# The last stage of a fused attention and two-layer kernel: two double steps split into single ones, two weight tiles loaded ahead, a new order

## The chip, the cores and the metric

The kernel runs on one core of a Trainium2 chip. The engines are named as in the profile: PE (TensorE, matrix products; PEld its weight loads), DVE (VectorE), ACT (ScalarE), POOL (GpSimd), and SP, whose queue issues the DMAs. The metric is the device time of one launch in microseconds (us): before the change 757.48 us, the median of three runs (756.21 to 758.75).

## The reference

Three stages follow one another: pooled attention, a soft mixture of experts, and a two-layer network with a bend between its layers. Only the last is touched:

```python
def _moe2_ref(x, w_in, w_out):          # x: 2304 x 512
    h = x @ w_in                        # w_in: 512 x 2048
    g = h - np.tanh(h)
    return (g @ w_out).astype(np.float32)   # w_out: 2048 x 512
```

The mixture before it gives `x = c @ slot_out` with 32 slots, so the kernel folds `slot_out @ w_in` into a 32-row matrix first, and h is c times that.

## The kernel before

**Tiling of the last stage.** The 2304 tokens are taken in 6 blocks of 384 (`TB`), the 2048 hidden columns in 16 tiles f of 128. A step is a block and two neighbouring tiles (`NF = 2`): 48 double steps. In the sequence `seq` they are numbered n = 0 to 47; the first block holds n = 0 to 7, the second begins with n = 8.

**One double step.** PE makes h for the two tiles (`fh`, line 1460, two products of 384 columns into one of two PSUM banks `h`). ACT reads h three times: its square u (`fu`, 1467), its tanh th (`ft`, 1470) and a mask big (`fb`, 1473), and makes y from u (`fy`, 1476). DVE multiplies u by th (`fm`, 1481), subtracts th from h (`fd`, 1484), makes a polynomial for small h (`fg`, 1487) and chooses between the two (`fp`, 1492). ACT rounds the result to gh (`fa`, 1495), DVE makes the remainder gl (`fl`, 1498). PE then adds to the three output tiles of the block (`acc`, 128 tokens each) the products gh with the upper half of a weight tile (o0), gh with its lower half (o1), and gl with the upper half (o2): 18 products of 512 columns (`fo`, line 1505). All five DVE instructions and all five ACT instructions of a double step are 768 columns wide. After the last step of a block an output tile is copied out by ACT or by DVE, whichever the planner finds free (`fe`, 1542 and 1544), and stored through SP (`fs`, 1548). The buffers u, y, m, th, big, gh and gl have three copies each, the banks h two, and there are four output accumulators, where a block needs three.

**What the later steps wait for.** The folded matrix (`s0`, `s1`) holds 16 tiles. Its first four come ready with the work just ahead (lines 1385 and 1386). The twelve others are made by `slot_rest` (line 1316: 24 products that read the converted weights i0 to i5), rounded by `s4` on ACT (1404), their remainder taken by `s5` on DVE (1407), and put in place by twelve small DMAs `s6` (1421): so h for f of 4 and above (`sw_done`) needs that whole chain. Only after all of the s6 does `reload` fetch the tiles 4 to 15 of the second weight.

**Loads ahead of it.** `top_up` (line 1082) hands memory that becomes free to the names in `wants`, in order, and issues the DMA that each needs: i0 to i5 at line 1103, the tiles of the second weight (numbers) at line 1105. c0 to c2, s0 and s1 are made on the chip and need none.

```python
wants = ["c0", "c1", "c2", "s0", "s1"] + [f"i{n}" for n in range(6)] + list(range(NF0))   # NF0 = 4
```

**Who sets the order.** `Plan.run` plays the stage through with a cost per operation and a delay between engines, at each free engine takes the ready operation with the lowest priority number, and writes the instructions in that order; on the chip each engine then runs its own list strictly in order. The priority is the step number plus an offset from `PO` by kind: h, u, t (th), b (big), y, m, d (th minus h), g, p, a (gh), l (gl), o0 to o2, ev (the copy out), r (slot_rest, s4, s5, s6). An operation that shares the bank h with another engine's (`alone`) waits until that one is done. `slot_rest` is held back until 4.0 us of planned time by `WAIT`.

```python
oh = op(pe(163 * NF), fh, q + PO["h"], deps=[...sw_done...], take=[hs], use=[hs])
om = op(dve(N), fm, q + PO["m"], deps=[ou, ot], take=[m], use=[u, th, m])
od = op(dve(N), fd, q + PO["d"], deps=[ot, om], use=[hs, th], alone=hs)
oe = op({**act(DM), **dve(DM)}, fe, q + PO["ev"], deps=outs[blk][t][-1:], take=[osb], use=[acc[t], osb])
```

Of the kernel before, what the change touches and what calls it, by code (L numbers as in the profile page):

```python
# [194 lines left out]
def fused_kernel(  # L195
# [12 lines left out]
    nc = tc.nc  # L208


    B, NP, _, S = q.shape
# [32 lines left out]
        "h": -8.11, "u": -2.9, "t": -2.69, "b": -2.37, "y": -2.66, "m": -13.37, "d": 0.89,  # L244
        "g": -5.49, "p": -3.56, "a": -1.55, "l": 2.75, "o0": 7.66, "o1": 8.11, "o2": 1.93,
        "ev": 5.8, "r": -0.78,
# [106 lines left out]
    def pe(ns):  # L353
        return {"PE": ns}
# [722 lines left out]
    wants = ["c0", "c1", "c2", "s0", "s1"] + [f"i{n}" for n in range(6)] + list(range(NF0))  # L1077
# [33 lines left out]
    with tc.manual_schedule():  # L1111
# [257 lines left out]
        seq = [(blk, f) for blk in range(NB) for f in range(0, KF, NF)]  # L1369
# [70 lines left out]
        def step(n):  # L1440
            blk, f = seq[n]
# [8 lines left out]
            def hp_():  # L1450
                return hs.tile[:, :, :TB]

            def v(sl, dt=None):
                t = sl.tile if dt is None else sl.tile.bitcast(dt)
                return t.rearrange("p (f c) -> p f c", f=NF)

            def fh(_):
                for k in range(NF):
# [16 lines left out]
            def fy(_):  # L1475
                nc.scalar.activation(
                    out=y.tile, in_=u.tile, func=AF.Square, scale=G_S, bias=gp[:, 0:1]
                )

            def fm(_):  # L1480
                nc.vector.tensor_tensor(out=m.tile, in0=u.tile, in1=th.tile, op=ALU.mult)  # L1481
# [4 lines left out]
            def fg(_):  # L1486
                nc.vector.scalar_tensor_tensor(
                    out=m.tile, in0=y.tile, scalar=G_Q, in1=m.tile, op0=ALU.add, op1=ALU.mult
                )

            def fp(_):
                nc.vector.copy_predicated(m.tile, big.tile.bitcast(U32), th.tile)  # L1492

            def fa(_):
                nc.scalar.activation(out=hi.tile, in_=m.tile, func=AF.Copy)  # L1495

            def fl(_):
                nc.vector.tensor_tensor(  # L1498
                    out=lo.tile, in0=m.tile, in1=hi.tile.bitcast(F32), op=ALU.subtract
                )  # L1500

            def fo(k, t):
                for x in range(NF):
                    l, c = ((hi, 0), (hi, DM), (lo, 0))[k]
                    nc.tensor.matmul(  # L1505
                        out=acc[t].tile, lhsT=l.tile[:, x * TB + t * 128:x * TB + (t + 1) * 128],
                        rhs=got[f + x][:, c:c + DM], start=(f == 0 and k == 0 and x == 0),
                        stop=(f == KF - NF and k == 2 and x == NF - 1),
                    )

            q = float(n)
            N = NF * TB
            oh = op(pe(163 * NF), fh, q + PO["h"], deps=[d for x in range(NF) for d in sw_done[f + x]],
# [11 lines left out]
            for k in range(3):  # L1525
                for t in range(NTB):
                    done = outs[blk][t]
                    deps = [ol if k == 2 else oa] + done[:1]
                    if f == KF - NF and k == 2:
                        deps += done  # L1530
                    o = op(pe(215.7 * NF), lambda _, k=k, t=t: fo(k, t),
# [4 lines left out]
            if f == KF - NF:  # L1536
# [73 lines left out]
```

## Time and profile before

| | |
|---|---|
| median of three runs | 757.48 us |
| profiled execution, its own time | 755.35 us |
| its span, first to last instruction | 753.6 us |
| PE busy | 726.4 us, 96% of the span |
| DVE busy | 652.8 us, 87% |
| ACT busy | 485.9 us, 64% |
| mean granted TensorE clock | 0.989 of full |
| start of the last stage (first h) | 519.39 us |
| last product of the last stage ends | 749.84 us |

The shares of the whole span hide that its stages differ; the last stage is 230 us of 753.6 and has to be read by itself. A window table gives the busy time of every engine in a stretch; the granted clock beside it says at which of its two levels (1.0 is 2.4 GHz, 0.5 is 1.2 GHz) PE worked there. The timeline lists the instructions by their start; neighbours of one kind are merged into one row, and the bracket at its end says how long the engine had been idle and what it waited for.

### The profile page before, as it was taken

How to read it: one execution, taken by the hardware profiler on the slowest of the kernel's cores; microseconds unless marked ns; L12 is line 12 of the kernel's file. 1: busy time of each engine (PE TensorE's matmuls, PEld its weight loads, DVE VectorE, ACT ScalarE, POOL GpSimd, SP SyncE). 2: the span in 40 equal slices, each digit the busy share in tenths (PEclk: the TensorE clock that was granted, in tenths of full speed). 3: DMA queues.
4: the chain of work that ended last, by engine and by line, in shares of the span. 5: the costliest groups of instructions: out<-in, count | busy, mean ns of one | idle time of the engine just before them, and what ended most of it. 6: DMA issues, size and time to landing. Idle time of an engine off the chain costs nothing.

```text
span 753.6 us, 16227 instructions
## 1 busy us (share of the span) xinstructions
PE 726.4 (96%) x5977; PEld 512.1 (68%) x5977; DVE 652.8 (87%) x1161; ACT 485.9 (64%) x1050; POOL 379.8 (50%) x275
## 2 busy tenths in 40 slices
PE   6999999999999989999989999998899999999998
PEld 3666666666666656666656666355678888888886
DVE  7999989898999999998989986513999999999994
ACT  1565666565666565666556666314878888888882
POOL 2699999969999869999939960000000000000000
PEclk9999999999999999999989999999799999999999
DMA  6445373453454444464444532999631010101001
GB/s 219 151 159 160 141 230 122 143 152 112 164 182 147 145 154 164 154 205 146 168 171 183 174 140 97 356 409 371 232 145 42 1 43 0 43 1 42 8 35 42
DMA packets 33551, 108.41 MB, mean 144 GB/s; under 512 B 5312, under 2 KB 6208, under 8 KB 33472
## 3 DMA queue, kind: packets, MB, share of 16 engines
q1 hardware_dynamic: 33472, 107.37, 40.5%
q8 instruction: 47, 0.77, 0.4%
q14 instruction: 32, 0.26, 0.1%
HBM read 90.24 MB, written 16.25 MB: 141 GB/s over the span
## 4 chain that ended last, share of the span: by engine, by line
PE 83%; DVE 7%; ACT 3%; POOL 3%; issue 2%; DMA 1%; SPq 0%; DVEq 0%; POOLq 0%; ACTq 0%
PE bk L1505 26%; PE bk L556 21%; PE bk L590 18%; PE bk L464 7%; POOL rt L609 3%; DVE mc L478 2%; PE h L1460 2%; PE bk L633 2%; PE bk L1330 2%; PE bk L1251 2%; DMA rt<-in_moe_w_in_dram 1%; PE bk L699 1%; PE bk L805 1%; PE bk L809 0%; DMA rt<-in_k_dram 0%
## 5 line engine op out<-in xcount | busy, mean ns | idle before, releaser
L609 POOL TENSOR_TENSOR rt<-rt 128x576 f32<-128x576 f32 x240 | 355.7, 1486 | 49.0 <-ACT rt L568 34.5
L568 ACT ACTIVATE rt<-bk 128x288 f32<-128x288 f32 x576 | 204.0, 412 | 147.1 <-PE bk L556 138.2
L478 DVE TENSOR_REDUCE mc<-bk 128x1 f32<-128x384 f32 x480 | 234.4, 546 | 26.3 <-PE bk L464 25.6
L556 PE MATMUL bk<-rt 64*128 64x288 f32 x1728 | 179.3, 310 | 4.8 <-DVE mc L478 4.6
L590 PE MATMUL bk<-rt 128*64 128x288 f32 x1152 | 173.3, 419 | 0.0
L556 PEld LDWEIGHTS bk<-rt 64*128 64x128 f32 x1728 | 138.8, 187 | 47.5 <-DVE mc L478 18.9
L1505 PE MATMUL bk<-rt,gh 128*128 128x512 f32 x576 | 145.3, 396 | 5.0 <-ACT gh L1495 5.0
L1505 PEld LDWEIGHTS bk<-rt,gh 128*128 128x128 f32 x576 | 109.4, 191 | 29.2 <-ACT gh L1495 6.7
L590 PEld LDWEIGHTS bk<-rt 128*64 128x64 f32 x1152 | 70.1, 136 | 55.7 <-issue 25.9
L464 PE MATMUL bk<-rt 64*128 64x384 f32 x480 | 100.1, 395 | 7.9 <-DVE rt L414 7.0
L556 PE MATMUL bk<-rt,one 64*128 64x288 f32 x576 | 91.0, 294 | 0.0
L464 PEld LDWEIGHTS bk<-rt 64*128 64x128 f32 x480 | 54.5, 194 | 47.3 <-issue 18.9
L1505 PE MATMUL bk<-rt,gl 128*128 128x512 f32 x288 | 81.8, 395 | 0.0
L1505 PEld LDWEIGHTS bk<-rt,gl 128*128 128x128 f32 x288 | 54.4, 191 | 9.9 <-DVE gl L1498 0.6
L556 PEld LDWEIGHTS bk<-rt,one 64*128 64x128 f32 x576 | 60.1, 187 | 0.0
L1467 ACT ACTIVATE u<-h 128x768 f32<-128x768 f32 x48 | 39.2, 816 | 27.9 <-PE h L1460 27.9
L1492 DVE COPY_PREDICATED m<-big,th 128x768 f32<-128x768 uint32 x48 | 51.4, 1070 | 0.0
L1481 DVE TENSOR_TENSOR m<-u,th 128x768 f32<-128x768 f32 x48 | 45.6, 951 | 6.4 <-ACT th L1470 6.3
L417 DVE TENSOR_TENSOR rt<-rt 128x576 fp32r<-128x576 f32 (+3 forms) x35 | 47.0, 1343 | 4.4 <-ACT rt L412 4.3
L1498 DVE TENSOR_TENSOR gl<-m,gh 128x768 fp32r<-128x768 f32 x48 | 45.7, 952 | 1.5 <-ACT gh L1495 1.5
L1484 DVE TENSOR_TENSOR th<-h,th 128x768 f32<-128x768 f32 x48 | 45.6, 951 | 0.0
L1495 ACT ACTIVATE gh<-m 128x768 fp32r<-128x768 f32 x48 | 40.9, 852 | 7.3 <-DVE m L1492 5.0
(136 smaller groups left out, 695.6 us busy)
## 6 DMA issues: line engine op xcount, KB each, us to landing
rt<-in_moe_w_dram SPq DMA_DIRECT2D x64, 512.0 KB
rt<-in_v_dram SPq DMA_DIRECT2D x16, 576.0 KB
rt<-in_k_dram SPq DMA_DIRECT2D x15, 576.0 KB
rt<-in_q_dram SPq DMA_DIRECT2D x15, 576.0 KB
rt<-in_moe_w_in_dram SPq DMA_DIRECT2D x16, 512.0 KB
rt<-in_moe_w_out_dram SPq DMA_DIRECT2D x16, 512.0 KB
wo_hl<-rt SPq DMA_DIRECT2D x16, 512.0 KB
rt<-wo_hl SPq DMA_DIRECT2D x16, 512.0 KB
```

The lines of the kernel that those rows point to most:

```text
L417: nc.vector.tensor_tensor(out=lo_t[:, c:end], in0=sl.tile[:, c:end], in1=hi_t.bitcast(F32)[:, c:end], op=ALU.subtract,)
L464: nc.tensor.matmul(out=ps.tile[:, :KW], lhsT=QH[a][lo:hi, q0:q0 + 128], rhs=KH[a][lo:hi, c0:c0 + KW],)
L478: nc.vector.tensor_reduce(out=msl.tile[:, n, g:g + 1], in_=ps.tile[:, :KW], axis=AX.X, op=ALU.max)
L556: nc.tensor.matmul(out=st.tile[:, :HQ], lhsT=w[lo:hi, k0:k0 + 128], rhs=x[lo:hi, q], start=(n == 0), stop=(n == 3),)
L568: nc.scalar.activation(out=psl.tile[:, h, :], in_=st.tile[:, :HQ], func=AF.Exp, scale=ESC)
L590: nc.tensor.matmul(out=pvs.tile[lo:hi, :HQ], lhsT=vt[:, cc, h, :], rhs=p.tile[:, h, :], start=(cc == 0), stop=(cc == NCH - 1),)
L609: eng.tensor_tensor(out=acc.tile, in0=p0.tile if c == 1 else acc.tile, in1=psl.tile, op=ALU.add)
L1481: nc.vector.tensor_tensor(out=m.tile, in0=u.tile, in1=th.tile, op=ALU.mult)
L1484: nc.vector.tensor_tensor(out=v(th), in0=hp_(), in1=v(th), op=ALU.subtract)
L1492: nc.vector.copy_predicated(m.tile, big.tile.bitcast(U32), th.tile)
L1498: nc.vector.tensor_tensor(out=lo.tile, in0=m.tile, in1=hi.tile.bitcast(F32), op=ALU.subtract)
L1505: nc.tensor.matmul(out=acc[t].tile, lhsT=l.tile[:, x * TB + t * 128:x * TB + (t + 1) * 128], rhs=got[f + x][:, c:c + DM], start=(f == 0 an ...
```

## The change

Four things change, all of them for the last stage.

- The sequence: the first double step (block 0, tiles 0 and 1) becomes two single ones, the last (block 5, tiles 14 and 15) as well: 50 steps for 48. A single step has instructions of 384 columns on ACT and DVE and takes nine output products. The priority's step number is now the position in hidden tiles divided by two, so the two singles stand at 0 and 0.5.
- In `wants`, the tiles 0 and 1 of the second weight come ahead of i0 to i5.
- The offsets `PO` are all new.
- The planner's cost of a product goes from 163 to 172 ns (h) and from 215.7 to 227 ns (o).

```diff
     PO = {
-        "h": -8.11, "u": -2.9, "t": -2.69, "b": -2.37, "y": -2.66, "m": -13.37, "d": 0.89,
-        "g": -5.49, "p": -3.56, "a": -1.55, "l": 2.75, "o0": 7.66, "o1": 8.11, "o2": 1.93,
-        "ev": 5.8, "r": -0.78,
+        "h": 0.13, "u": -2.03, "t": -15.26, "b": -1.63, "y": -11.63, "m": -23.28, "d": 13.36,
+        "g": 3.69, "p": -8.99, "a": -7.63, "l": 4.72, "o0": 6.44, "o1": 8.34, "o2": 7.72,
+        "ev": 15.23, "r": -0.3,
     }
...
-    wants = ["c0", "c1", "c2", "s0", "s1"] + [f"i{n}" for n in range(6)] + list(range(NF0))
+    wants = ["c0", "c1", "c2", "s0", "s1", 0, 1] + [f"i{n}" for n in range(6)] + list(range(2, NF0))
...
-        seq = [(blk, f) for blk in range(NB) for f in range(0, KF, NF)]
+
+        seq = [(blk, f, NF) for blk in range(NB) for f in range(0, KF, NF)]
+        seq = [(0, 0, 1), (0, 1, 1)] + seq[1:-1] + [(NB - 1, KF - 2, 1), (NB - 1, KF - 1, 1)]
...
-            q = float(n)
-            N = NF * TB
-            oh = op(pe(163 * NF), fh, q + PO["h"], deps=[d for x in range(NF) for d in sw_done[f + x]],
+            q = float(blk * KF + f) / NF
+            oh = op(pe(172 * nf), fh, q + PO["h"], deps=[d for x in range(nf) for d in sw_done[f + x]],
...
-                    o = op(pe(215.7 * NF), lambda _, k=k, t=t: fo(k, t),
+                    o = op(pe(227 * nf), lambda _, k=k, t=t: fo(k, t),
                            q + PO[f"o{k}"] + (2 if n == len(seq) - 1 else 0.01) * t, deps=deps,
```

The rest of the diff makes the instructions of a step as wide as the step (`N = nf * TB` columns of the same buffers).

## Rows read from the trace of the kernel before

**Rows 1.** The page, part 1: busy time and share of the span by engine.
```profile
PE 726.4 (96%) x5977; PEld 512.1 (68%) x5977; DVE 652.8 (87%) x1161; ACT 485.9 (64%) x1050; POOL 379.8 (50%) x275
```
**Rows 2.** Chain of waits, last stage: start us, us, what.
```profile
622.79 0.35 PE h L1460 x2
623.14 4.10 PE bk L1505 x18
...
733.03 16.81 PE bk L1505 x74
```
**Rows 3.** Windows, last stage: stretch, its length, busy by engine, clock, DMA share, GB/s.
```profile
519.39:526.80 7.41, 5.72 (x30) 2.31 (x30) 5.47 (x8) 7.09 (x11) 0.00 (x0) 1.00 0.89 352
526.80:540.77 13.97, 11.27 (x42) 8.80 (x42) 13.39 (x16) 10.94 (x16) 0.00 (x0) 0.88 0.52 152
540.77:554.34 13.57, 11.97 (x37) 8.30 (x37) 12.71 (x15) 10.39 (x15) 0.00 (x0) 0.75 0.91 367
554.34:743.60 189.26, 189.26 (x850) 158.34 (x851) 184.23 (x208) 159.34 (x217) 0.00 (x0) 1.00 0.06 22
```
**Rows 4.** Windows of line 1505 alone (PE, PEld, clock, DMA, GB/s).
```profile
554.34:749.90 195.56, 188.33 (x798) 149.19 (x798) 1.00 0.06 22
```
**Rows 5.** Timeline, 519 to 546 us: start, us, engine, line, operation, count, idle before.
```profile
519.39 0.66 PE L1460 MATMUL h<-rt 128*128 128x384 f32 x2
...
520.82 3.99 PE L1316 MATMUL bk<-rt,acc_s 128*32 128x512 f32 x24
...
522.50 0.18 PEld L1316 LDWEIGHTS bk<-rt,acc_s 128*32 128x32 f32 x3 [0.25 <-DMA rt<-wi_c]
...
524.74 0.61 PE L1460 MATMUL h<-rt 128*128 128x384 f32 x2
...
526.82 1.20 PE L1505 MATMUL bk<-rt,gh 128*128 128x512 f32 x4 [1.48 <-ACT gh L1495]
...
527.26 8.22 SPq L1421 DMA_DIRECT2D rt<-sh  x12
...
528.58 1.01 PE L1460 MATMUL h<-rt 128*128 128x384 f32 x2 [0.56 <-DVE th L1484]
...
531.10 0.68 DVE L1407 TENSOR_TENSOR sh<-bk,sh 96x512 fp32r<-96x512 f32 x1
...
535.53 9.63 SPq L1105 DMA_DIRECT2D rt<-wo_hl  x12
...
536.41 0.51 PE L1460 MATMUL h<-rt 128*128 128x384 f32 x2
...
544.92 0.88 ACT L1495 ACTIVATE gh<-m 128x768 fp32r<-128x768 f32 x1
```
**Rows 6.** Windows, all engines: the DMA-bound stretch and the two at half clock.
```profile
504.00:525.00 21.00, 19.14 (x408) 13.76 (x398) 5.97 (x15) 5.80 (x10) 0.00 (x0) 1.00 1.03 408
...
528.35:531.65 3.30, 3.07 (x8) 2.60 (x9) 3.30 (x5) 2.36 (x4) 0.00 (x0) 0.50 0.43 99
541.97:548.39 6.42, 6.05 (x13) 4.18 (x14) 6.41 (x9) 6.07 (x9) 0.00 (x0) 0.50 1.03 416
```
**Rows 7.** Timeline, a settled step: m of one double step and of the next.
```profile
721.71 0.95 DVE L1481 TENSOR_TENSOR m<-u,th 128x768 f32<-128x768 f32 x1
...
726.14 0.94 DVE L1481 TENSOR_TENSOR m<-u,th 128x768 f32<-128x768 f32 x1
```
**Rows 8.** Groups by line and shape: 384 columns on DVE and on ACT.
```profile
L417 DVE TENSOR_TENSOR rt<-rt 128x384 fp32r<-128x384 f32 x3 | 1.7, 559 | 4.4 <-ACT rt L412 4.3
...
L412 ACT ACTIVATE rt<-rt 128x384 fp32r<-128x384 f32 x3 | 1.6, 522 | 1.9 <-DMA rt<-in_k_dram 1.8
```
**Rows 9.** Timeline: the last stores.
```profile
719.29 31.53 SPq L1548 DMA_DIRECT2D out_dram<-osb  x4
```
**Rows 10.** Groups by line: the copy out, on ACT and on DVE.
```profile
L1544 ACT ACTIVATE osb<-bk 128x512 f32<-128x512 f32 x17 | 9.7, 612 | 6.4 <-PE bk L1505 6.4
...
L1542 DVE COPY osb<-bk 128x512 f32<-128x512 f32 x1 | 0.7, 673 | 0.0
```

More of the change, by code (lines that the diff above doesn't have):

```diff
@@ L1440, in step @@
         def step(n):
-            blk, f = seq[n]
+            blk, f, nf = seq[n]
+            N = nf * TB
             hs = hbank()
@@ L1450, in hp_, with w @@
             def hp_():
-                return hs.tile[:, :, :TB]
+                return hs.tile[:, :nf, :TB]
             def v(sl, dt=None):
                 t = sl.tile if dt is None else sl.tile.bitcast(dt)
-                return t.rearrange("p (f c) -> p f c", f=NF)
+                return t[:, :N].rearrange("p (f c) -> p f c", f=nf)
+            def w(sl, dt=None):
+                return (sl.tile if dt is None else sl.tile.bitcast(dt))[:, :N]
             def fh(_):
-                for k in range(NF):
+                for k in range(nf):
                     x = f + k
@@ L1476, in fy @@
                 nc.scalar.activation(
-                    out=y.tile, in_=u.tile, func=AF.Square, scale=G_S, bias=gp[:, 0:1]
+                    out=w(y), in_=w(u), func=AF.Square, scale=G_S, bias=gp[:, 0:1]
                 )
             def fm(_):
-                nc.vector.tensor_tensor(out=m.tile, in0=u.tile, in1=th.tile, op=ALU.mult)
+                nc.vector.tensor_tensor(out=w(m), in0=w(u), in1=w(th), op=ALU.mult)
             def fd(_):
@@ L1487, in fg @@
                 nc.vector.scalar_tensor_tensor(
-                    out=m.tile, in0=y.tile, scalar=G_Q, in1=m.tile, op0=ALU.add, op1=ALU.mult
+                    out=w(m), in0=w(y), scalar=G_Q, in1=w(m), op0=ALU.add, op1=ALU.mult
                 )
             def fp(_):
-                nc.vector.copy_predicated(m.tile, big.tile.bitcast(U32), th.tile)
+                nc.vector.copy_predicated(w(m), w(big, U32), w(th))
             def fa(_):
-                nc.scalar.activation(out=hi.tile, in_=m.tile, func=AF.Copy)
+                nc.scalar.activation(out=w(hi), in_=w(m), func=AF.Copy)
             def fl(_):
                 nc.vector.tensor_tensor(
-                    out=lo.tile, in0=m.tile, in1=hi.tile.bitcast(F32), op=ALU.subtract
+                    out=w(lo), in0=w(m), in1=w(hi, F32), op=ALU.subtract
                 )
             def fo(k, t):
-                for x in range(NF):
+                for x in range(nf):
                     l, c = ((hi, 0), (hi, DM), (lo, 0))[k]
@@ L1507, in fo @@
                         rhs=got[f + x][:, c:c + DM], start=(f == 0 and k == 0 and x == 0),
-                        stop=(f == KF - NF and k == 2 and x == NF - 1),
+                        stop=(f + nf == KF and k == 2 and x == nf - 1),
                     )
-            q = float(n)
-            N = NF * TB
-            oh = op(pe(163 * NF), fh, q + PO["h"], deps=[d for x in range(NF) for d in sw_done[f + x]],
+            q = float(blk * KF + f) / NF
+            oh = op(pe(172 * nf), fh, q + PO["h"], deps=[d for x in range(nf) for d in sw_done[f + x]],
                     take=[hs], use=[hs])
@@ L1528, in step @@
                     deps = [ol if k == 2 else oa] + done[:1]
-                    if f == KF - NF and k == 2:
+                    if f + nf == KF and k == 2:
                         deps += done
-                    o = op(pe(215.7 * NF), lambda _, k=k, t=t: fo(k, t),
+                    o = op(pe(227 * nf), lambda _, k=k, t=t: fo(k, t),
                            q + PO[f"o{k}"] + (2 if n == len(seq) - 1 else 0.01) * t, deps=deps,
@@ L1535, in step @@
                     done.append(o)
-            if f == KF - NF:
+            if f + nf == KF:
                 for t in range(NTB):
```

## The prediction

> **What bounds the kernel now.** I read the page first: PE is busy for 96% of the span [rows 1]. That is an average over stages, so the last stage comes next. Its chain of waits, from 554 us on, is PE alone, without a gap: 18 output products in 4.10 us (0.228 us each) and a pair of h products in 0.35 us, so 4.45 us per double step, up to the last product at 733.03 + 16.81 = 749.84 us [rows 2]. The windows say the same: in 554.34 to 743.60 PE is busy for 189.26 of 189.26 us [rows 3]. After 554.34 the stage can gain only if less PE work is left there. Of the 864 products 798 lie after that moment [rows 4], so only 66 are done in the first 35 us.
>
> How large is that loss? The stage's PE work at full speed is 864 x 0.228 = 196.8, 48 pairs x 0.345 = 16.6, and slot_rest 4.0 [rows 5], together 217.4 us. The stage took 749.84 - 519.39 = 230.4 [rows 2, 5]. So 13.0 us are lost, all in the ramp. Idle PE makes (7.41 - 5.72) + (13.97 - 11.27) + (13.57 - 11.97) = 6.0 of it [rows 3]. Half clock, 1.2 GHz in two stretches with 3.07 + 6.05 us of busy PE, makes half of that, 4.6 [rows 6]; both stretches follow idle time. The other 2.4 is products spaced wider than 0.228.
>
> Why the ramp starves is seen in the timeline [rows 5]. The first output product waits until 526.82 for gh, 7.4 us after the first h. The h for f = 4 comes only at 536.41: slot_rest runs at 520.82 to 524.81, the first s6 goes out at 527.26, the s5 that half of them need runs at 531.10, and the twelve take SP until 535.48. Meanwhile steps of the second block fill ACT and DVE (the h at 524.74, and one more), but three accumulators belong to the first block and only one is left for theirs. DVE is busy for 13.39 of 13.97 us there [rows 3], partly with results PE can't use yet, and the gh of f = 4 is ready only at 544.92 + 0.88 = 545.8.
>
> DVE is the second bound, and a close one. From one m to the next pass 726.14 - 721.71 = 4.43 us [rows 7], against PE's 4.45. It runs ahead now only because PE lost 13 us.
>
> **The change part by part.** All sums are in the time of the profiled execution, whose 755.35 us are 753.6 of span and 1.75 around it; it lies 2.1 below the median of the runs, and I carry the difference in us over to that median.
>
> *Two single steps at the start.* A DVE instruction of 384 columns takes 0.56 us and one of 768 0.95 [rows 7, 8]; on ACT a 384 takes 0.52 [rows 8] against 0.88 for a 768 [rows 5]. In the chain h, u, th, m, g, d, p, gh one h product goes (0.33), three ACT instructions lose 0.35 each and four DVE instructions 0.39: 2.9 us, so the first gh is ready near 524 rather than 526.8. It brings PE less than that, because slot_rest stands ahead of it in PE's list (next part). The price is more fixed time: back to back, a 768 on DVE takes 4.43 / 5 = 0.886 a piece, 0.07 less than its duration, so two halves take 2 x (0.56 - 0.07) - 0.89 = 0.09 more; ten such pairs (five each at start and end) are 0.9 us on DVE. ACT is idle for 30 of 189 us [rows 3] and hides its own. The bounds are 0 (pairs hidden where DVE idles) and 10 x (2 x 0.56 - 0.95) = 1.7.
>
> A rule speaks against it: the Trainium skill, VectorE: DVE Perf Modes, section on the TRN2 errata, says that each VectorE instruction pays a fixed latency once, and advises tiles of at least 512 elements; its (N + 151) / 0.96 ns gives 0.557 and 0.957 us, which agrees with 0.559 and 0.95 here. By it the ten pairs would cost 10 x 0.157 = 1.6 us in place of 0.9.
>
> *Two single steps at the end.* PE has the same 18 products there and is the bound; the copy out, the store and the 3.8 us from the last product to the end of the span stay. I cost it at nothing; if DVE is late at the end, half-size steps save up to about 1.5 us of the last chain (p, gh, gl halved), if not they cost the 0.45 already counted.
>
> *Two tiles loaded sooner.* The DMA engines are full from 504 to 525 us at 408 GB/s [rows 6], so what is put ahead of i0 to i5 delays them by 2 x 0.524 MB / 408 GB/s = 2.57 us. slot_rest waited for the last of them at 522.50 [rows 5]; now that is 525.07, and its end moves from 524.81 to 527.4. Nothing hides this from the s4-s5-s6 chain. In return tiles 0 and 1 are there before 524; where they were, they could have come close to that. So the edit by itself loses; bounds 0 (slot_rest is late for another reason) to 2.57, and I take 2.57. PE's list, by the planner's own costs, becomes: both single h, then the h of tiles 2 and 3 (the first bank comes free at about 2.9 us of planned time, slot_rest at 4.06), then slot_rest, then gh products of both singles. So PE idles from 520 to 523 and partly to 525, and from 527.4 on it has work.
>
> *The order.* Offsets -0.3 for s4 and s5 against 3.7 to 13.4 for g, l, d: s5 should follow s4 by one instruction, not by four. With s4 at 527.5 and s5 by 529.3, the first four s6 (0.6 us each, the order on SP unchanged) are out by 530.5. A DMA takes up to 753.6 - 750.82 + 0.33 = 3.1 us from issue to done, by the last store [rows 9]; a small one I put at 2.3. So h for f = 4 at about 533, bounds 532 and 536.5. By the planner's costs only one step of the second block now comes ahead of it. DVE then has, from 521.0: 4.9 (singles), 4.4 (tiles 2 and 3), 0.7 (s5), 4.4 (second block), 3.6 (m, g, d, p for f = 4), and ACT 0.9: gh of f = 4 near 540, where it was at 545.8. The reload begins at 528 + 12 x 0.61 = 535.3 as before, and its first two tiles land two tile times (2.6) and some 2 us later, at 539.9: the same moment. Until then PE has 36 + 6 products and five pairs of h, 11.3 us from 527.4, so it is busy until 538.7.
>
> *The sum.* At 540.0 there are 42 products and six pairs done. 822 x 0.228 + 42 x 0.345 = 201.7 are left: PE's end at 741.7. For half clock after the idle time near 521 I add 1.7 (half of a 3.3 us stretch; bounds 0 and 3.2, half of the longer one [rows 6]). DVE's own end: 521.0 + 48 x 4.43 + 0.9 + 0.7 + 3 idle in the ramp + 2 for the last products = 740.2. The two are now so close that each delay of either reaches PE, where the lead hid them: DVE's idle time in the settled part was 5.0 of 189 us [rows 3], and I let a third, 1.6, count. PE's end: 745.0, a gain of 4.8, say 5.0 us: 750.4 for a profiled execution, 757.48 - 5.0 = 752.5 for the median.
>
> **The rivals.**
>
> *The ramp only changes its shape.* If s5 keeps its old distance, the h for f = 4 follows slot_rest by 536.41 - 524.81 = 11.6 us: at 539.0, and gh 5.3 later (five DVE instructions and gh), at 544.3. PE then idles for 5 us, gets a second stretch of half clock (3.2), and ends at 544.3 + 201.7 + 3.2 = 749.2, with some of the 1.6 at 750: no change. For it: nothing of the chain is shortened but its priorities. Against it: s5 was delayed by four DVE instructions that now rank behind it.
>
> *DVE becomes the bound through the copies out* (slower). The new offset for ev, 15.23, ranks the copy of an output tile behind every ACT instruction of the next steps, but on DVE before d (13.36) of steps two and more ahead. A copy on DVE costs 0.67 [rows 10], and one of 18 was there. If all 18 went there, DVE would end at 740.2 + 18 x 0.67 = 752.3, with the hiccups at 753.9: 4.0 us slower, 761.5. It decides from (749.8 - 741.8) / 0.67 = 12 copies. Against it: ACT is free for 30 of 189 us, 0.7 per step [rows 3], and the planner takes whichever engine is free first.
>
> *The full gain.* If slot_rest isn't late (or gh of the singles goes ahead of it) and nothing stumbles, DVE's 740.2 is the end: 9.6 us faster, 747.9. Against it: DVE and PE would have to mesh for 48 steps with 0.02 us to spare in each.
>
> **How the numbers follow.** Forecast 0.55, the ramp of another shape 0.22, copies on DVE 0.17, full gain 0.06. What can be told from no change is 0.3%, 2.3 us. Forecast and full gain are faster: 0.61; the second is the same: 0.22; the third slower: 0.17. The forecast's own range, by its bounds (slot_rest 2.57, clock 3.2, hiccups 0 to 5), is 749.5 to 755.2. The range takes in most of the second case and the lower part of the slower one: 747.8 to 759.5.
>
> **What would show it.** Right: the first output product not before 527; s5 within 2 us of s4; h for f = 4 (the first after the s6) near 533; over 80 products done by 554; PE gapless from 541, its last product near 745. Wrong: slot_rest ending before 525.5 (the loads did not matter); gh of f = 4 after 543; DVE with more than a handful of copies; idle PE between 560 and 730 of more than 3 us in sum.

## The result, and the profile after

The change makes the kernel slower: 761.74 us (median of four runs; 761.10 to 762.10) against 758.05 of the kernel before, run beside it; ratio 1.0051, 95% interval 1.0031 to 1.0070. The forecast was 752.5 us, with a chance of 0.61 for faster.

The profiled execution took 761.54 us, 6.2 more than the 755.35 before. The first h of the last stage comes 3.4 us later (522.84 for 519.39), the stage takes 232.6 us for 230.4, and from its last product to the end of the span it is 4.4 us for 3.8. The 3.4 can't be put down to the change: the kernel before, profiled a second time (e0 below), had its first h at 521.17, and e17 below, which differs from it in the planner's costs alone, at 523.47.

The page of the changed kernel, part 1, beside [rows 1]: PE is busy 3.2 us longer for the same number of products.

```profile
PE 729.6 (96%) x5977; PEld 510.6 (67%) x5977; DVE 656.9 (86%) x1173; ACT 485.9 (64%) x1058; POOL 380.2 (50%) x275
```

Windows of its last stage, columns as in [rows 3]. The first three are the ramp, then two short stretches in it, and the part after the first 35 us.

```profile
522.84:532.46 9.62, 7.20 (x29) 2.77 (x29) 7.68 (x14) 7.54 (x15) 0.00 (x0) 0.82 0.63 251
532.46:543.20 10.74, 9.59 (x43) 7.65 (x43) 8.66 (x11) 8.90 (x13) 0.00 (x0) 1.00 0.41 104
543.20:554.94 11.74, 8.70 (x31) 6.57 (x31) 10.38 (x12) 8.16 (x12) 0.00 (x0) 0.85 0.99 384
528.00:530.00 2.00, 2.00 (x12) 0.95 (x9) 2.00 (x4) 2.00 (x4) 0.00 (x0) 0.50 0.38 147
548.00:551.00 3.00, 3.00 (x8) 2.33 (x8) 3.00 (x5) 1.06 (x2) 0.00 (x0) 0.50 1.01 408
...
557.80:755.39 197.59, 197.49 (x873) 160.91 (x871) 188.41 (x218) 160.91 (x225) 0.00 (x0) 1.00 0.06 22
```

In the ramp PE idles 2.42 + 1.15 + 3.04 = 6.6 us, as long as before (6.0), and again has two stretches at half clock. The last row is the surprise: PE looks busy for 197.49 of 197.59 us. The same window for line 1511 alone, the products, shows that it isn't well busy:

```profile
557.80:755.39 197.59, 187.84 (x793) 147.70 (x791) 1.00 0.06 22
```

793 products are left after 35 us, so 71 are done; before it was 66. At 0.2278 us a product and 0.345 us a pair of h (40 pairs, the other 80 PE instructions) the work is 180.65 + 13.80 = 194.45 us: 3.1 us are lost. The same sum for the kernel before, over 554.40 to 749.79 with the 798 products of [rows 4] and 39 pairs, gives 195.39 - 181.78 - 13.46 = 0.15. I call this figure the loss after 35 us. (The Trainium skill, Perfetto Trace Analysis, section Identifying the Most-Contended Engine, says that the busy share of the matmuls is not a good measure of how close a kernel is to roofline. This trace agrees: 99.9% busy, and 1.6% lost.) The chain of waits shows where it hides: beside the even 4.10 and 0.35 of [rows 2] stand pairs of h that take 0.53 and 0.58.

```profile
585.74 0.35 PE h L1466 x2
586.09 3.19 PE bk L1511 x14
589.28 0.53 PE h L1466 x2
589.80 7.29 PE bk L1511 x32
...
597.13 0.58 PE h L1466 x2
```

The waits from 557.8 on (us in total, times, the longest) name the cause of most: the weight load of h waits for the subtraction on DVE that frees its bank ("DVE th"), or it waits for nothing that the profile shows ("issue"), behind the 39 semaphore instructions that stand at this line.

```profile
PEld h L1466 <- issue: 3.2, 9, 0.4
...
PEld h L1466 <- DVE th L1490: 1.2, 4, 0.4
PEld bk L1511 <- DVE osb L1547: 0.5, 2, 0.3
...
```

The timeline of the ramp, beside [rows 5] (h of f = 4 is the one at 537.28, its gh the one at 545.99):

```profile
522.84 0.66 PE L1466 MATMUL h<-rt 128*128 128x384 f32 x2
...
525.91 0.62 PE L1466 MATMUL h<-rt 128*128 128x384 f32 x2 [2.42 <-DVE th L1490]
...
526.46 6.06 PE L1316 MATMUL bk<-rt,acc_s 128*32 128x512 f32 x24
...
527.21 0.38 PEld L1316 LDWEIGHTS bk<-rt,acc_s 128*32 128x32 f32 x6 [0.60 <-DMA rt<-wi_c]
...
532.46 1.65 PE L1511 MATMUL bk<-rt,gh 128*128 128x512 f32 x6
532.56 0.60 ACT L1406 ACTIVATE sh<-bk 96x512 fp32r<-96x512 f32 x1 [2.07 <-PE bk L1316]
533.18 7.63 SPq L1423 DMA_DIRECT2D rt<-sh  x12
533.19 0.69 DVE L1409 TENSOR_TENSOR sh<-bk,sh 96x512 fp32r<-96x512 f32 x1 [1.23 <-ACT sh L1406]
...
537.28 0.53 PE L1466 MATMUL h<-rt 128*128 128x384 f32 x2
...
543.20 0.62 PE L1466 MATMUL h<-rt 128*128 128x384 f32 x2 [1.15 <-DVE th L1490]
...
545.99 0.85 ACT L1501 ACTIVATE gh<-m 128x768 fp32r<-128x768 f32 x1
...
546.72 0.72 PE L1511 MATMUL bk<-rt,gl 128*128 128x512 f32 x2 [1.98 <-DVE gl L1504]
```

PE waits for DVE at the third h, slot_rest stands behind that h and runs partly at half clock (6.06 us for 3.99), s5 makes DVE wait 1.23 us for s4, and after 542 PE stands still three more times.

### The profile page after: what moved, and what is told of

Same layout as the page of the kernel before. It is cut to its first block, busy times and chain, and to the rows that moved or that the text cites. A ratio compares the mean times of both kernels' runs of the same rounds, so it can differ in the third digit from the quotient of the medians.

```text
span 759.8 us, 16244 instructions
## 1 busy us (share of the span) xinstructions
PE 729.6 (96%) x5977; PEld 510.6 (67%) x5977; DVE 656.9 (86%) x1173; ACT 485.9 (64%) x1058; POOL 380.2 (50%) x275
## 4 chain that ended last, share of the span: by engine, by line
PE 42%; DMA 5%; DVE 3%; ACT 2%; issue 1%; ACTq 0%; DVEq 0%; SPq 0%
PE bk L1511 25%; PE bk L556 5%; PE bk L590 5%; DMA rt<-in_moe_w_dram 4%; PE h L1466 2%; PE bk L464 1%; DMA rt<-wi_c 1%; PE bk L1316 1%; DVE mc L478 1%; PE bk L1251 1%; PE bk L633 1%; PE bk L805 0%; PE bk L809 0%; ACT th L1476 0%; DVE m L1487 0%
## 5 line engine op out<-in xcount | busy, mean ns | idle before, releaser
L478 DVE TENSOR_REDUCE mc<-bk 128x1 f32<-128x384 f32 x480 | 234.7, 549 | 28.4 <-PE bk L464 27.8
L1511 PEld LDWEIGHTS bk<-rt,gh 128*128 128x128 f32 x576 | 107.8, 189 | 24.6 <-ACT gh L1501 1.4
L464 PEld LDWEIGHTS bk<-rt 64*128 64x128 f32 x480 | 55.2, 194 | 46.9 <-issue 20.6
L1511 PE MATMUL bk<-rt,gl 128*128 128x512 f32 x288 | 80.1, 395 | 2.0 <-DVE gl L1504 2.0
L1476 ACT ACTIVATE th<-h 128x768 f32<-128x768 f32 (+1 forms) x50 | 39.7, 797 | 26.3 <-PE h L1466 26.1
L417 DVE TENSOR_TENSOR rt<-rt 128x576 fp32r<-128x576 f32 (+3 forms) x35 | 48.8, 1396 | 4.6 <-ACT rt L412 4.5
L1498 DVE COPY_PREDICATED m<-big,th 128x768 f32<-128x768 uint32 (+1 forms) x50 | 50.5, 1032 | 0.0
L1487 DVE TENSOR_TENSOR m<-u,th 128x768 f32<-128x768 f32 (+1 forms) x50 | 45.9, 918 | 3.2 <-ACT u L1473 2.2
L1504 DVE TENSOR_TENSOR gl<-m,gh 128x768 fp32r<-128x768 f32 (+1 forms) x50 | 45.5, 917 | 2.7 <-ACT gh L1501 2.7
L1482 ACT ACTIVATE y<-u,gp 128x768 f32<-128x768 f32 (+1 forms) x50 | 46.5, 930 | 0.0
L1490 DVE TENSOR_TENSOR th<-h,th 128x768 f32<-128x768 f32 (+1 forms) x50 | 45.0, 918 | 1.3
```

Source lines behind the costliest of these rows:

```text
L417: nc.vector.tensor_tensor(out=lo_t[:, c:end], in0=sl.tile[:, c:end], in1=hi_t.bitcast(F32)[:, c:end], op=ALU.subtract,)
L464: nc.tensor.matmul(out=ps.tile[:, :KW], lhsT=QH[a][lo:hi, q0:q0 + 128], rhs=KH[a][lo:hi, c0:c0 + KW],)
L478: nc.vector.tensor_reduce(out=msl.tile[:, n, g:g + 1], in_=ps.tile[:, :KW], axis=AX.X, op=ALU.max)
L1482: nc.scalar.activation(out=w(y), in_=w(u), func=AF.Square, scale=G_S, bias=gp[:, 0:1])
L1487: nc.vector.tensor_tensor(out=w(m), in0=w(u), in1=w(th), op=ALU.mult)
L1498: nc.vector.copy_predicated(w(m), w(big, U32), w(th))
```

## The experiments

All ratios are against the kernel before, run on the same chip beside the kernel. "Stage + tail" is from the first h to the end of the span in one profiled execution.

| kernel | clock, first 35 us | products by 35 us | loss after 35 us | stage + tail, us | ratio, 95% interval |
|---|---|---|---|---|---|
| before; again (e0) | 0.85; 0.90 | 66; 70 | 0.15; -0.2 | 234.2; 232.9 | 1 |
| the changed kernel | 0.90 | 71 | 3.1 | 237.0 | 1.0051 (1.0031 to 1.0070) |
| e7, before + new loads | 0.90 | 70 | -0.2 | 232.8 | 0.9986 (0.9970 to 1.0002) |
| e12, before + new costs | 0.95 | 71 | 2.8 | 235.6 | 1.0037 (1.0021 to 1.0053) |
| e5, changed, old offsets and costs | 0.85 | 64 | 0.9 | 236.0 | 1.0023 (1.0003 to 1.0043) |
| e2, changed, old offsets | 0.90 | 67 | 2.5 | 236.9 | 1.0055 (1.0038 to 1.0073) |
| e17, e12 + DVE's measured cost | 0.95 | 73 | 0.7 | 233.2 | 1.0004 (0.9990 to 1.0018) |
| e9, searched order | 0.90 | 82 | -0.05 | 230.6 | 0.9960 (0.9945 to 0.9975) |
| e16, e9 + true PE costs | 0.95 | 84 | 2.2 | 232.1 | 0.9987 (0.9972 to 1.0002) |
| e18, e16 + DVE's measured cost | 0.90 | 80 | 0.2 | 231.1 | 0.9963 (0.9950 to 0.9976) |
| e15, changed, costs 3% less | 0.85 | 68 | 1.5 | 235.9 | 1.0020 (1.0003 to 1.0037) |
| e14, changed, old costs | 0.90 | 73 | 10.0 | 243.4 | 1.0137 (1.0115 to 1.0159) |
| e19, changed, DVE's measured cost | 0.85 | 60 | 4.0 | 240.3 | 1.0103 (1.0084 to 1.0123) |
| e1, changed, old loads | 0.95 | 81 | 3.3 | 234.9 | 1.0031 (1.0016 to 1.0047) |
| e6, e1 + slot_rest first | 0.95 | 83 | 3.5 | 234.7 | 1.0044 (1.0026 to 1.0062) |
| e8, new order, true costs | 0.95 | 81 | 2.5 | 233.7 | 0.9997 (0.9983 to 1.0012) |
| e4, changed, d early | 0.90 | 75 | 2.8 | 235.4 | 1.0038 (1.0023 to 1.0052) |
| e3, changed, all steps double | 0.95 | 72 | 6.7 | 239.3 | 1.0085 (1.0067 to 1.0104) |
| e13, changed, last step double | 0.90 | 72 | 3.1 | 236.1 | one execution |

The count by 35 us has the granted clock in it too: 0.05 of the clock over 35 us is 1.75 us of work at full speed, at 4.45 us for 18 products and their h up to 7 products (an estimate). At the same clock of 0.90 the changed kernel's 71 products stand beside 70 of e0 and 70 of e7, so its ramp gains nothing, while e9 (82) and e18 (80) gain ten.

### The edits one at a time

**e7_loads_alone**: the new loads in the kernel before.

```diff
-    wants = ["c0", "c1", "c2", "s0", "s1"] + [f"i{n}" for n in range(6)] + list(range(NF0))
+    wants = ["c0", "c1", "c2", "s0", "s1", 0, 1] + [f"i{n}" for n in range(6)] + list(range(2, NF0))
```


> The kernel before with the new load order alone: tiles 0 and 1 of the second weight ahead of i0 to i5. Theory (the loads delay slot_rest by 2.57 us and with it all of the ramp): slot_rest ends near 8 after the first h (before: 5.4), the h of f = 4 comes 1.5 to 2.5 us later than the 17.0 of before, ratio 1.002 to 1.0033. Rival (s4 and s5 stood 1.8 and 4.5 us behind their inputs in their engines' lists anyway, so there is room): no change, within 0.7 us.

Timeline of e7 (first h at 522.22):

```profile
526.58 3.62 PE L1316 MATMUL bk<-rt,acc_s 128*32 128x512 f32 x20 [1.51 <-DMA rt<-wi_c]
...
533.98 0.68 DVE L1407 TENSOR_TENSOR sh<-bk,sh 96x512 fp32r<-96x512 f32 x1
```

slot_rest waits 1.51 us for its loads and ends 8.0 us after the first h instead of 5.4, the delay that the prediction had worked out. But s5 starts 11.76 us after the first h, where it did before (531.10 - 519.39 = 11.71, [rows 5]): DVE had other work ahead of it in its list. The delay costs nothing: the rival was right, and the theory, which is the prediction's own price, fell.

**e12_true_costs**: the new planner costs in the kernel before.

```diff
-            oh = op(pe(163 * NF), fh, ...
+            oh = op(pe(172 * NF), fh, ...
...
-                    o = op(pe(215.7 * NF), ...
+                    o = op(pe(227 * NF), ...
```


> The kernel before, with one edit: the planner's costs of a product are 172 and 227 ns instead of 163 and 215.7 (offsets, loads and sequence as before). Theory (slack): the shorter costs make the plan run ahead of PE, so that on the chip whatever PE needs is there when PE comes to it; with the measured costs the plan is only as late as the chip and every jitter reaches PE. Then PE loses 2 to 4 us after the first 35 us of the stage (0.15 in the kernel before), h pairs of over 0.45 us show up there, and the time is 1.002 to 1.005 of the kernel before. Rival (the offsets do it): with the old offsets the costs hardly change the order, the loss stays under 0.8 us and the ratio is 0.999 to 1.001.

Its waits from 557 us on, and a piece of its chain:

```profile
PEld bk L1505 <- DVE gl L1498: 1.9, 7, 0.5
PEld h L1460 <- DVE th L1484: 1.2, 3, 0.4
PEld bk L1505 <- ACT gh L1495: 0.5, 1, 0.5
```
```profile
608.84 0.34 PE h L1460 x2
609.18 3.65 PE bk L1505 x16
612.83 0.60 PE h L1460 x2
```

The theory's numbers came: loss 2.8, an h pair of 0.60, ratio 1.0037. Two numbers that run nothing on the chip, but only tell the planner what a product takes, cost 0.37% with the order of the kernel before, as against 0.51% for the whole change.

**e2_old_offsets** and **e5_old_costs**: the changed kernel with the old offsets, and with the old costs as well.

```diff
-        "h": 0.13, "u": -2.03, "t": -15.26, "b": -1.63, "y": -11.63, "m": -23.28, "d": 13.36,
+        "h": -8.11, "u": -2.9, "t": -2.69, "b": -2.37, "y": -2.66, "m": -13.37, "d": 0.89,
...
```


> The changed kernel with the old offsets PO (single steps, new load order and new costs stay). Theory (the new offsets lose time in the settled part, where PE waits at h for the bank): from 38 us after the first h on PE runs without the 2 to 3 us of extra waiting, the stage from first h to last product is about 231 us (changed: 232.6; before: 230.5), the kernel 1 to 2 us faster than the changed one. Rival (the single steps are what costs, through their fixed time): as slow as the changed kernel or slower, stage 232.6 or more.

> As e2 (single steps, new load order, old offsets) but with the planner's old costs of a product, 163 and 215.7 ns, too: the change without its order. Up to 35 us after the first h e2 had 67 products done, and from there it lost 2.5 us against 0.228 us per product and 0.345 per pair of h, though its offsets were those of before, which lost 0.15. Theory (the old costs, 5% too short, made the planner place each product on PE as if PE were faster than it is, so on the chip what it needs is always there; the true costs take that slack away): the loss after 35 us falls under 0.8, the kernel is 2 us faster than e2, ratio about 1.0025. Rival (the loss comes from the single steps or from PE's smaller lag): as e2, 1.0055.

The waits of e2 after 35 us are those of e12, nearly to the row, with 0.7 us of "issue" beside them:

```profile
PEld bk L1511 <- DVE gl L1504: 1.7, 7, 0.5
PEld h L1466 <- DVE th L1490: 1.2, 3, 0.4
...
PEld bk L1511 <- ACT gh L1501: 0.5, 1, 0.5
```

So e2's theory fell (the old offsets do not help), and its rival's time came without its cause: e5 has the same single steps, and loses 0.9 us after 35 us where e2 loses 2.5. e5's own theory came in its ratio, and just missed its loss (0.9 for under 0.8).

With the old offsets the four corners are there: neither edit 1, new costs alone 1.0037, single steps and loads alone 1.0023 (e5), all of them 1.0055 (e2). The costs bring 0.32 to 0.37%, single steps with loads 0.18 to 0.23%, and the new offsets, from e2 to the changed kernel, nothing that can be told (1.0055 to 1.0051). The part of single steps with loads is hardly clear of noise: the interval of e5 begins at 1.0003, and those of e12 and e2 overlap. For the costs, e12's interval begins at 1.0021, while those of e5 and e2 just overlap.

### Why true costs hurt

By the kernel's own figures the planner takes a step's PE work as 18 x 215.7 + 2 x 163 = 4.21 us with the old costs and 4.43 with the new; on the chip it is 4.45 [rows 2]. Its DVE work it takes as 5 x 867 ns = 4.335 us in both; on the chip it is 4.43 [rows 7], 2.2% more. So with the old costs PE is the engine that comes late against the plan; with the new ones DVE is.

**e17_true_both**, and the same in two other kernels, **e18_searched_true_both** and **e19_after_true_both**:

```diff
-            om = op(dve(N), fm, ...
+            om = op(dve(N + 18), fm, ...
...
```


> The kernel of e12_true_costs (the kernel before with 172 and 227 ns a product, loss of 2.8 us after 35 us), and beside it the planner's cost of a 768-column DVE instruction of the stage raised from 867 to 886 ns, which is what the trace shows (4.43 us a step over five). Theory (the two engines' costs against each other): the plan takes DVE 2.2% too short; with PE's costs 5% too short as well, PE comes late against the plan and DVE's products are always there; with PE's costs alone made true, PE comes on time and DVE late. With both true the loss falls from 2.8 to under 1.2 us, ratio 0.997 to 1.002. Rival (PE has to be planned too short, whatever DVE's cost): loss stays at 2 to 4 us, ratio 1.002 to 1.006.

> The kernel of e16_searched_true_costs (the searched order with 172 and 227 ns, loss of 2.2 us after 35 us, ratio 0.9987), with the planner's DVE cost at 886 ns as in e17. Theory (the costs against each other): the loss goes to under 0.6 us and the ratio to 0.994 to 0.9975, as in e9_searched. Rival (PE has to be planned too short): loss stays at 1.5 us or more, ratio 0.998 to 1.002.

> The changed kernel with the planner's DVE cost of the 768- and 384-column instructions raised by 19 ns each as in e17, nothing else. Theory (the costs against each other): its loss falls from 3.1 to 1 to 2.5 us; the offsets were not chosen for these costs, so the ramp may lose what the rest gains: ratio 1.001 to 1.007. Rival (PE has to be planned too short): loss of 3 us or more and ratio as in the changed kernel or higher, 1.004 to 1.009.

**e9_searched**, an order searched anew with double steps, old loads, `WAIT` 1533 and costs 2% under the measured ones, and **e16_searched_true_costs**, the same with the measured ones:

> Double steps throughout and the loads in the order of the kernel before; slot_rest held back until 1.533 us instead of 4.0; costs of 168.6 and 222.6 ns, 2% under the measured ones; offsets searched anew so that h for f = 4 comes early and nothing after the ramp waits. Theory (the ramp can be gained if the slack is kept): over 76 products by 35 us after the first h (66 in the kernel before), a loss of under 1 us after that, and 2 to 4 us less in all: ratio 0.9945 to 0.998. Rival (DVE lies so close to PE that any earlier ramp is given back): over 76 products, but a loss of 2.5 us or more after 35 us, ratio 0.999 to 1.002.

> The kernel of e9_searched (loss of 0 after 35 us) with the measured costs of 172 and 227 ns in place of 168.6 and 222.6, nothing else. Theory (slack): 2% are what separates no loss from a loss of 2.5 to 4 us, the gain of 3.0 us goes, ratio 0.999 to 1.002. Rival (it was the offsets that made e9_searched good): loss under 1 us, ratio under 0.998.

PE's own waits after 35 us in e16, and then in e18, where this is the only row left:

```profile
PEld bk L1510 <- DVE gl L1503: 1.8, 7, 0.5
PEld h L1465 <- DVE th L1489: 1.4, 4, 0.4
PEld h L1465 <- issue: 0.8, 3, 0.3
```
```profile
PEld h L1465 <- DVE th L1489: 0.2, 1, 0.2
```

DVE's measured cost takes the loss from 2.8 to 0.7 (e12 to e17; the intervals of the ratios don't meet) and from 2.2 to 0.2 (e16 to e18; they just overlap). e16 itself stays just below the theory's figures (2.2 for 2.5 to 4, 0.9987 for 0.999 to 1.002), far from its rival's loss. So PE need not be planned too short: in these two orders what counts is that the plan doesn't take DVE for faster, against PE, than it is. e14 below shows that this isn't enough in every order: its plan has DVE's work at 4.335 us a step against 4.21 for PE's, and it loses 10 us. e9 (PE 2% short, DVE 2.2%) has no loss and is, at 3.0 us less than the kernel before, the best kernel of this study, beside e18.

**e14_only_costs_back** and **e15_costs_97**: the changed kernel with 163 and 215.7, or 167 and 221, in place of 172 and 227.

> The changed kernel with one edit undone: the planner's costs of a product are 163 and 215.7 ns again (its offsets, single steps and loads stay). Theory (slack by itself): costs 5% under the measured ones protect any order, so the loss after the first 35 us falls from 3.1 us to under 1, and the ratio from 1.0051 to 1.002 or less. Rival (costs and offsets belong together): the new offsets make a good order only with the costs that they stand with; with 5% shorter ones the plan's PE runs ahead of the plan's ACT and DVE, which lie close to it, the order takes h and products at other places, and PE waits for gh and gl for more than 4 us after 35 us: ratio over 1.006.

> The changed kernel with the planner's costs of a product at 167 and 221 ns, 3% under its 172 and 227, and nothing else. Theory (slack by itself): the loss after 35 us lies between that of the changed kernel (3.1) and nothing, at 0.5 to 2 us, the ramp as it was (about 71 products), and the ratio at 1.001 to 1.004. Rival (any other cost makes an order that does not fit): loss of 4 us or more, ratio over 1.006.

```profile
PEld bk L1511 <- ACT gh L1501: 8.7, 7, 2.9
```
```profile
569.72 2.77 PE L1511 MATMUL bk<-rt,gh 128*128 128x512 f32 x8 [2.58 <-ACT gh L1501]
```

Above are a row of the waits and one of the timeline of e14: PE now comes to products whose gh is up to 2.9 us late. The slack theory by itself is wrong here and its rival right: offsets make a good order only with the costs that they were chosen with. e15, 3% under, behaves as the theory says. e19 lies outside both ranges in its time, and its loss after 35 us (4.0) is in the rival's range, not in the theory's. But that stretch has a piece of the ramp in it: PE stands still for 3.04 us for a gh at 557.94, is at clock 0.75 in 557.70 to 564.50, and has only 60 products by 35 us. Here are the products from 41.85 us after the first h on, in e19 and then in the changed kernel:

```profile
564.50:758.69 194.19, 186.11 (x786) 146.07 (x784) 1.00 0.06 21
```
```profile
564.69:755.41 190.72, 181.34 (x766) 142.65 (x764) 1.00 0.06 21
```

The loss is 194.19 - 786 x 0.2278 - 39 x 0.345 = 1.7 us in e19, and 190.72 - 766 x 0.2278 - 38 x 0.345 = 3.1 in the changed kernel. DVE's measured cost takes nearly half of the settled loss away there too; the ramp is what its order spoils.

### The ramp and the single steps

**e1_old_loads** (the changed kernel with the old `wants`), **e6_rest_first** (e1 with slot_rest held back to 1.5 us of planned time instead of 4.0) and **e8_new_order** (single steps at the start only, old loads, offsets searched with the true costs, `WAIT` 1887):

```diff
-    WAIT, NF0 = 4000.0, 4
+    WAIT, NF0 = 1500.0, 4
```


> The changed kernel, with the tiles 0 and 1 of the second weight loaded behind i0 to i5 again. In the changed kernel slot_rest began 3.6 us after the first h and ended 9.7 after it (before: 5.4). Theory (the loads hardly matter, since slot_rest now stands in PE's list behind the h of tiles 2 and 3, which waits for a bank until 3.1 us, and its slowness is half clock): slot_rest still begins at 3.6 and ends at 9.1 or later, the stage is at most 0.6 us shorter, the time within 1 us of the changed kernel's 761.7. Rival (the loads delay the whole ramp, as predicted): slot_rest ends 2.6 us sooner, at 7.1, and the kernel is 2.6 us faster, 759.1.

> As e1 (the change with the old load order) with WAIT at 1500 for 4000, so that slot_rest stands in PE's list ahead of the h of tiles 2 and 3, as it did before the change; the planner's order behind it shifts. In e1 PE idled for 2.4 us ahead of that h, then ran slot_rest in 5.3 us at half clock, where before it took 4.0; it ended 9.0 after the first h. Theory (that order of the two costs the ramp about 2 us): slot_rest ends by 6, at least 88 products are done at 35 us (e1: 81), the kernel is 1.5 to 2 us faster than e1, ratio about 1.001. Rival (the gh of f = 4 comes from DVE, which works without a pause, so slot_rest's time does not matter): no change, 1.003.

> A version that takes what the runs so far favour: single steps at the start only, the old load order, slot_rest ahead of the third h (WAIT 1887), and other offsets (d 3.8, b -1.68, u -6.83, o0 to o2 at 4.83, 5.77, 8.76), with the new costs of a product. Theory (the ramp carries the loss and can be shortened): at 35 us at least 95 products are done (before: 66), 4 to 7 us won there, of which 2 to 3 are lost again after it, as in all kernels with the true costs; ratio 0.994 to 0.997. Rival (what the ramp wins is all given back where PE waits for DVE): ratio 0.999 to 1.001.

Old loads give 10 products more by 35 us, though slot_rest ends only 0.7 us sooner after the first h (9.0 for 9.7); the ratios' intervals overlap. Neither account of e1 came whole: the stage is 2.1 us shorter (230.5), not 0.6 at most, and slot_rest does not end at 7.1. With slot_rest in front (its end at 5.4) hardly more products are done (83 for 81, forecast 88) and no time is won, as e6's rival has it. All three still lose 2.5 to 3.5 us later on; e8 misses its theory (81 products for 95) and, with 11 to 15 products more than the kernel before, is no faster than it, as its rival has it.

**e4_d_early** (`"d"` back from 13.36 to 0.89), **e3_no_singles** (the line with the single steps left out) and **e13_last_double** (only the last step double again):

```diff
-        seq = [(0, 0, 1), (0, 1, 1)] + seq[1:-1] + [(NB - 1, KF - 2, 1), (NB - 1, KF - 1, 1)]
+        seq = [(0, 0, 1), (0, 1, 1)] + seq[1:]
```


> The changed kernel with the offset of d (th minus h, the last reader of a bank) back from 13.36 to 0.89, nothing else. In the changed kernel the weight loads of h stood idle for 9.0 us waiting for d and 3.3 more without a visible cause; before it was 3.3 and 0. Theory (the late d keeps the bank and PE, which is the bound, waits for it): these fall to under 5 us together, the settled part is 2 to 2.5 us shorter, the kernel about 759.5. Rival (the settled loss comes from another place, such as copies out on DVE, or d is only where the planner had time left): no change, 761 to 762.

> The changed kernel with double steps throughout (new offsets, loads and costs stay). Theory (the single steps at the start help the ramp by what the first gh comes sooner, 2.9 us at most, and cost at the end 0.6 through stores that queue up): the kernel is 1 to 3 us slower than the changed one, 763 to 765. Rival (the halves' fixed time, 0.9 to 1.7 us on DVE, is the loss): 1 to 1.5 us faster, 760.5.

> The changed kernel with its last step left double; the two single steps at the start stay, and so do loads, offsets and costs. Theory: the last single step bunches the three copies and stores behind its nine products, and the tail from the last product to the end of the span is 4.4 us for that; with the double step it is 3.8 or less, as before, and the stage (first h to last product) stays within 0.5 us of the changed kernel's 232.6. Rival (the tail has to do with the order of ev): it stays at 4.4.

An early d takes the "issue" waits from 3.2 to 0.5 us, and "DVE th" grows from 1.2 to 3.2: it looks like one wait in two forms, and the loss stays at 2.8, so the theory's 2 to 2.5 us did not come. e3's time is that of its theory (1 to 3 us slower), but not by its mechanism: it has 72 products by 35 us, one more than with the single steps, and loses 6.7 us later on. It says less than it seems, for like e14 it takes the offsets out of the setting they were chosen for. e13 does answer, as its theory has it: the tail falls from 4.4 to 3.8 us. The ends of the two kernels, the changed one first; the last row of each is a window of all engines:

```profile
754.08 1.96 ACT L1549 ACTIVATE osb<-bk 128x512 f32<-128x512 f32 x3 [4.91 <-PE bk L1511]
...
754.71 1.69 SPq L1553 DMA_DIRECT2D out_dram<-osb  x3
755.02 0.39 PE L1511 MATMUL bk<-rt,gl 128*128 128x512 f32 x1
...
755.50:758.30 2.80, 0.00 (x0) 0.00 (x0) 0.00 (x0) 0.54 (x1) 0.00 (x0) 1.00 0.76 284
```
```profile
753.84 3.05 SPq L1553 DMA_DIRECT2D out_dram<-osb  x3
...
755.29 0.61 PE L1511 MATMUL bk<-rt,gl 128*128 128x512 f32 x2
755.94 0.60 ACT L1549 ACTIVATE osb<-bk 128x512 f32<-128x512 f32 x1 [0.76 <-PE bk L1511]
...
756.85:757.38 0.53, 0.00 (x0) 0.00 (x0) 0.00 (x0) 0.00 (x0) 0.00 (x0) 1.00 0.00 0
```

With nine products in the last step its tiles are done 0.68 us apart, with eighteen 1.36. The issue of the last store ends 1.0 us after the last product in both kernels (754.71 + 1.69 = 756.40 after 755.41, and 753.84 + 3.05 = 756.89 after 755.90), so it isn't the issues that queue. From there to the end of the span it is 3.4 us in the changed kernel and 2.8 in e13: the three stores move at 284 GB/s on average there, one behind the other, while in e13 nothing is moved for 0.53 us ahead of the last.

**e0_before_again**: the kernel before, unchanged.

> The kernel before, unchanged, profiled once more. In its first profiled execution the mixture's first weights w1 are used at 478.0 us, in the changed kernel and in all experiments at 479.2 to 481.4, though the instructions up to there are the same. Theory (execution to execution): this one starts at 479 or later too, and its stage still takes 230.4 us (within 0.4) with a tail of 3.8. Rival (the changed kernels delay the attention by something that the trace does not name): 478.0 again.

```profile
521.20:556.20 35.00, 28.74 (x114) 19.31 (x115) 32.76 (x39) 29.72 (x42) 0.00 (x0) 0.90 0.75 275
556.20:750.29 194.09, 194.09 (x872) 162.07 (x870) 182.91 (x206) 159.20 (x218) 0.00 (x0) 1.00 0.06 22
```

w1 came at 479.1 us, not 478.0, as the theory has it; but the stage took 229.1 us, outside of the 230.4 within 0.4 that it gave: in the first 35 us the clock was 0.90 where the first profile had 0.85 (519.40 to 554.40), and 70 products were done. So a difference of four products by 35 us is within what one kernel does by itself.

## Why the prediction was wrong

**What bounds the kernel: right.** DVE as a close second bound, behind PE's lead, was the right reading; its consequence was priced too low.

**The failed step is the sum's ramp**: "At 540.0 there are 42 products and six pairs done", and from there a gapless PE. An end at 745.0 with 1.6 us of hiccups means 225.6 us of stage and, after 35 us, 190.6 = 1.6 + 39.5 pairs (13.6) + 770 products: 94 done. It was 71. The 23 missing products are 5.2 us, three quarters of the 7.0 between 225.6 and 232.6. Six of them are missing at that mark, 20.6 us after the first h, where the changed kernel has done as many products as the kernel before (windows of the products alone, the changed kernel first):

```profile
522.84:543.44 20.60, 9.02 (x36) 6.65 (x36) 0.92 0.52 176
```
```profile
519.39:539.99 20.60, 9.93 (x36) 7.60 (x36) 0.92 0.64 219
```

The other 17 are missing from the 14.4 us behind it, where the sum had PE without a gap. Of its parts:

- slot_rest was to end 8.0 us after the first h and ended 9.7 after. Its place behind the third h was right; half clock while it ran was in the sum only as a lump behind.
- s5 within 2 us of s4: right (0.63). It blocks DVE for 1.23 us, with p of tiles 2 and 3 waiting behind it, which I had not seen.
- h of f = 4 was to come 13.6 us after the first h: it came 14.4 after. Nearly right.
- gh of f = 4 was to be ready near 540, 20.6 after: it ended 24.0 after (546.84), past the 543 that I had named as the mark of a wrong forecast. From its h on DVE had the second block's instructions in between, and idled for what ACT had not made (0.44 and 0.30 us).
- "Until then PE has 36 + 6 products and five pairs of h" and "gapless from 541": PE stood still at 543.20 (1.15), 546.72 (1.98) and 554.94 (1.06), and had a second stretch at half clock, 548 to 551, where the sum had 1.7 us for one.

That is the first rival's picture ("the ramp only changes its shape"), of whose 5 us of idle PE 4.2 came (1.15 + 1.98 + 1.06), with its second half clock, though by other means than a distant s5.

**The hiccups, 1.6 us, were mis-sized**: 3.1. I saw that DVE and PE step within 0.02 us of each other, but the fourth edit, the planner's new costs, has no term in the sum and no rival: it stands at nothing without a reason. e12 and e16 show losses of 2.8 and 2.2 us with PE's costs made true, and e17 and e18 how DVE's cost takes most of them away. For the changed kernel's own 3.1 us the evidence is thinner: e15 and e19 about halve it (1.5, and 1.7 in the settled part), e14 makes it larger, and where the other half comes from stays open. The sign that I had named, idle PE of more than 3 us, would not have found it: PE was idle for 0.1.

**How the slowdown adds up.** Stage and tail are 237.0 us, 2.8 and 4.1 more than in the two executions of the kernel before (234.2 and 232.9), around the 3.7 between the medians. In both comparisons 3.0 to 3.3 us are the loss after 35 us and 0.6 is the tail; the ramp gives 0.8 back against the first, whose clock was 0.85, and nothing against the second. So 1.3 of the 13.0 us that the sum set out to win back were that execution's own.

**Two tiles loaded sooner, "the edit by itself loses", 2.57 us**: the delay was exact (2.6 in e7), its price was not: s5 stood behind four DVE instructions anyway. I had named them in the first rival, and yet wrote that nothing hides the delay. In the changed order, where s5 comes at once, slot_rest ends only 0.7 us sooner without it (e1); e1 gains 10 products, of which up to 7 can be the clock (0.95 there, 0.90 in the changed kernel).

**Single steps.** At the end "I cost it at nothing": 0.6 us in the tail. At the start: the 384-column instructions take 0.54 to 0.58 us on DVE, as estimated from [rows 8], and follow one another every 0.47 (five from 526.24 to 528.58) where the sum had 0.49; by that ten pairs cost about 0.5 us of DVE, where the sum had 0.9. (The formula of the Trainium skill, VectorE: DVE Perf Modes, section on the TRN2 errata, gives 0.557 for the duration, from which the prediction drew a cost of 1.6. This trace nearly agrees on the duration, with 0.546 for m, but not on the cost, which goes by the spacing.) The first gh was ready 5.0 us after the first h (527.33 + 0.52 - 522.84), where the forecast had 4.6 and the kernel before 7.4: nearly right. Ahead of it stood more than the sum had: ACT makes th of both singles before the first u, and on DVE an m of the second comes before p of the first. But PE's first product came 9.6 us after the first h (532.46; before 7.4), behind slot_rest, so what was won in the chain brought PE nothing.

**Copies on DVE**: three, where that rival needed twelve. It fell, and that its 761.5 us lie beside the measured 761.74 is chance: the slower side came true by another mechanism, the one I had under "full gain, against it".

Open: why in the changed kernel the offsets gain nothing in the ramp, beyond the places named; half of its loss after 35 us; and the split between single steps at the start and loads, which e5 holds together.

## What to carry to other kernels

A planner's costs matter by their ratio: where two engines lie within a per cent of each other, as here, correcting one engine's cost and leaving the other's 2% short turned hidden waits into visible ones in two orders, and offsets searched with one set of costs were worth little with another (e14). A window in which the bound engine is "busy" all the time can still lose per cents; divide the work that it did by the price of one, and compare. Before a delay is priced, look at what already stands in front of its consumer on that engine's own list.

## What the runs showed of the hardware that was not expected

- The ramp's half clock differs between executions of one kernel: 0.85 and 0.90 over the first 35 us, 66 and 70 products, 1.3 us of stage.
- Both times in the changed kernel it came after PE had taken up work again: PE resumed at 525.91 after 2.42 us idle and the clock was 0.50 in 528 to 530; it resumed at 546.72 after 1.98 idle and was at 0.50 in 548 to 551.
- The spread of one kernel's runs goes with the clock. In the 110 runs of the kernel before that stand beside the experiments, the median is 758.83 us where the run's mean granted clock is 0.986 (40 runs), 758.11 at 0.989 (22 runs) and 756.28 at 0.991 (36 runs). Whether an order changes how often this happens is open; in the pairs e12 and e17, e16 and e18 the mean clock of the runs differs by less than 0.001.
- Small waits of a weight load for the bank don't show as idle PE: the pair takes 0.5 to 0.6 us instead of 0.345, and the busy time grows.
